# Attention beside an MLP on one core: the wide exponential of the turned head moved behind the third or fourth pair of scores

## The chip, the core and the metric

The kernel runs on one core of a Trainium2 chip. The core has five engines, each with a queue of its own that is worked off in order: PE (TensorE, matmuls), DVE (VectorE), ACT (ScalarE), POOL (GpSimd) and SP (SyncE, which here only issues DMAs). POOL and ACT issue DMAs too. Matmuls write to PSUM, eight banks of 128 x 512 float32; everything else lies in SBUF or in DRAM.

The metric is the device time of one execution in microseconds (us). The median of three runs is 1149.64 us (1147.74 to 1149.71). The profile was taken from one execution, which took 1147.51 us.

## The reference

```python
x = A_x                                   # 1 x 2048 x 448
xn = _layernorm(x, axis=-1)
# attention, 16 heads of 28, one key and one value head for all
q = (xn @ wq) ; k = xn @ wk ; v = xn @ wv
p = softmax(q k^T * 28**-0.5)             # 16 x 2048 x 2048
a = (p v) @ wo
# channel MLP: layernorm again, 448 -> 1792 -> 448
h = gelu(einsum("bsd,df->bsf", _layernorm(xn), w1) + b1)
return x + a + (einsum("bsf,fd->bsd", h, w2) + b2)
```

All data are float32. Products that need it are split into a high and a low part.

## The kernel before, in words

**Order of the whole.** First come the layer norm, the projections to q, k and v, and the MLP, with the attention's row maxima woven in (up to about 470 us). The rest of the span is the attention proper. All of it is written out by hand: the program is recorded in the order in which the Python code runs, engine by engine, and no scheduler changes that order.

**Units and steps.** The attention has 16 units u: four chunks c of 512 queries by four groups g of four heads. A unit has 8 steps, one for each pair of key tiles kt, kt + 1 (128 keys each). So there are 128 steps n, and n = 8u + kt/2.

**Two ways to compute p = exp(score).** Heads 0 to 2 of a unit (in units 0 and 1 all four) are computed with keys on the partitions. `scores` (L780 to L793) makes two matmuls of 128 x 512 into one two-bank PSUM tile `s` of a pool with two buffers, and one ACT instruction takes the exponential of both (128 x 1024, L793). That is "a pair". The maximum over keys must be known before, and is folded into the matmul as an additional row of the queries. It comes from `max_stream` (L475 on): one matmul (L485) and one DVE reduction (L486) for each 128 queries by 512 keys, 16 for each head computed so, 800 in all. These matmuls take buffers of the PSUM pool `mp`, tiles `m`, of which there are three.

Head 3 of units 2 to 15 (`TURNED`) is computed the other way round, with queries on the partitions. `turned_scores` (L736 on) makes a matmul of 128 x 512 into a tile `m` (L742); DVE scales it into the SBUF tile `raw` and takes the maximum on the way (L743). Four of these make one tile t of 128 queries by 2048 keys, and L747 joins the four maxima. `turned_exp` (L753 to L765) then takes a wide exponential in place (128 x 1024, L760; two for each tile t) and issues eight DMAs of 64 KB that put blocks of 32 x 32 in order in the tile `turned`: three from POOL's queue, five from SP's. `turn_blocks` (L767 to L770) transposes within the blocks on DVE (128 x 1024, L769) and so gives the same p, keys on the partitions, for two key tiles. A turned head has 16 turned matmuls, 8 wide exponentials and 8 transpositions. The first transposition of a unit needs the data of all eight wide exponentials.

**Value products.** `pv` (L717 on) multiplies p with v: for each key tile one matmul per head (L722), the four heads side by side in the columns. They run in bursts of two key tiles, one burst a step, and always those of the step before. At the end of a unit `norm_jobs` (L649 on) divides by the sums of the softmax, in stages that later steps call one by one (ACT, DMAs on POOL's queue, DVE, POOL). At the end of a chunk `o_jobs` (L629 on) multiplies by `wo`, 12 matmuls a step for four steps.

**The order in a step.** `ORDERS` (L28) spells it out, a string for units 0 and 1 and one for the others. Each letter is a call:

- `p`: one pair of scores. In turned units there are three pairs a step, in units 0 and 1 four.
- `m`: one maximum of `max_stream`, if the plan says that it is due. The plan spreads what is left of the 800 over the steps by `weight` (L805).
- `t`: one turned matmul with its DVE instruction, from a given step on.
- `x`: one wide exponential with its eight DMAs, if a tile t is complete.
- `T`: one transposition.
- `P`: the burst of value products.
- `e`: in a given step of a unit, `load_max`: the finished maxima of the next unit are transposed and loaded.
- `n`: one stage of `norm_jobs`. `o`: one tile of `o_jobs`.

From step 8 on the queries of a later unit (`load_q`, L447 on, DMAs L457), the queries for the maxima and for the turned heads (`load_m`, L404 on, DMAs L409) and the stages of `norm_jobs` are loaded through POOL's queue. `load_q` is called at the start of a unit's first step.

Tiles of p come from a pool of seven buffers, `turned` from one of two, `raw` from one of three.

Of the kernel before, what the change touches and what calls it, by code (L numbers as in the profile page):

```python
# [24 lines left out]
SCALE = DH ** -0.5  # L25
BURST = 2
MLP_MAX = 20
ORDERS = ("mptmpmtmpmexnPpmonm", "ptmpTeoxnPptmTn")  # L28
TURNED = tuple(range(2, 16))
RAWS = 3  # L30
LEAD = 11
# [5 lines left out]
def block_kernel(ctx, tc, x, wq, wk, wv, wo, w1, b1, w2, b2, out):  # L37
# [4 lines left out]
    def f(t):  # L42
        return t.bitcast(F32)
# [7 lines left out]
    def heads_of(u):  # L51
        return 3 if u in TURNED else 4
# [346 lines left out]
    NU = len(units)  # L399
# [16 lines left out]
    for c in range(NCH):  # L416
        center, turn = norm_parts((c + 1) % NCH, c + 1 == NCH)
        for i in range(4):
# [7 lines left out]
            if i in ((2, 3) if c == 0 else (1, 3)):  # L426
                n = 2 * c + i // 3
# [19 lines left out]
    def load_q(u):  # L447
        c, g = units[u]
        cols = slice(c * CW, (c + 1) * CW)
        if u < 2:  # L450
            qst.append(xt_p.tile([P, 4, CW], F32R, name="xh"))
            pool.memset(f(qst[u]), 0.0)
        qs = qst[u % 2]
        for blk, i in ((1, 0), (2, 0), (0, 1), (3, 1)):
            nh = heads_of(u)
            src = qd[i][4 * DH * g:4 * DH * g + DH * nh, cols].rearrange("(j r) n -> r j n", r=DH)
            loads.dma_start(f(qs[32 * blk:32 * blk + DH, 0:nh, :]), src)  # L457
        qss[u] = qs
# [5 lines left out]
    def load_max(u):  # L464
        qs, mr = qss[u], mrs.pop(u)
        nh = heads_of(u)
        pm = mtile([nh * CT, P])
        pe.transpose(pm, mr[:, 0:nh * CT], ident)
        mn = keep.tile([4 * CT, 2, P], F32R, name="mn", bufs=1)[0:nh * CT]
        act.activation(mn[:, 0, :], pm, AF.Copy, scale=-1.0)  # L470
        dve.scalar_tensor_tensor(mn[:, 1, :], pm, -1.0, f(mn[:, 0, :]), op0=ALU.mult, op1=ALU.subtract)
        loads.dma_start(f(qs[60:61, 0:nh, :]), f(mn[:, 0, :]))
        loads.dma_start(f(qs[124:125, 0:nh, :]), f(mn[:, 1, :]))
# [128 lines left out]
    def turned_tile():  # L602
        return att.tile([P, 4 * CT, CW], F32, name="turned", bufs=2)
# [14 lines left out]
    def prep_wo(g):  # L618
        act.activation(woh[:, g, :], wor[:, g, :], AF.Copy)
        pool.tensor_sub(wol[:, g, :], wor[:, g, :], f(woh[:, g, :]))  # L620
# [8 lines left out]
    def o_jobs(c, gs, tiles=range(CT)):  # L629
        last = NG - 1 in gs  # L630
        for k in tiles:
            po = mtile([P, D])
            ts = slice(k * P, (k + 1) * P)
            for g in gs:
                oth, otl = ots[c, g]
                pe.matmul(po, oth[:, ts], woh[:, g, :], start=(g == gs[0]), stop=False)  # L636
                pe.matmul(po, oth[:, ts], wol[:, g, :], start=False, stop=False)
                pe.matmul(po, otl[:, ts], woh[:, g, :], start=False, stop=(g == gs[-1]))
            a = rows[c, k]
            dve.tensor_add(a, a, po)  # L640
            if last:
                (nc.scalar if k % 2 and c == NCH - 1 else nc.sync).dma_start(ov[:, CT * c + k, :], a)
            yield
# [73 lines left out]
    def pv(u, kt):  # L717
        if kt == 0:
            pos[u] = op.tile([P, CW], F32, name="po")
        po = pos[u]  # L720
        for j in range(4):
            pe.matmul(po[32 * j:32 * j + 32, :], vs[:, kt, :], ps.pop((u, kt, j)),  # L722
                      start=(kt == 0), stop=(kt == NT - 1))
        if kt == NT - 1:
            if u == NU - 1:
                end_jobs(u, pos.pop(u))
                return
            side.add(norm_jobs(u, pos.pop(u)))
            side.step()
            c, g = units[u]  # L730
            if c < NCH - 1 and g == NG - 1:
                oside.add(o_wait(c, range(NG), range(CT)))
# [20 lines left out]
    def turned_exp():  # L753
        if not exps:
            return
        u, t, raw, m3, h = exps.pop(0)
        if u not in turned:
            turned[u] = turned_tile()
        rs = slice(2 * h, 2 * h + 2)
        act.activation(raw[:, rs], raw[:, rs], AF.Exp, bias=m3[:, 4:5], scale=1.0)  # L760
        for r in range(2 * h, 2 * h + 2):
            for a in range(4):
                q = pool if a == 3 or (a == 2 and r % 2) else nc.sync
                q.dma_start(turned[u][32 * r:32 * r + 32, 4 * t + a, :],  # L764
                            raw[32 * a:32 * a + 32, r].rearrange("p b i -> p (b i)"))  # L765

    def turn_blocks(u, kt):  # L767
        p = pair_of()
        dve.transpose(p.rearrange("p k (g j) -> p g k j", j=32),  # L769
                      turned[u][:, :, 32 * kt:32 * kt + 64].rearrange("p g (k j) -> p g k j", j=32))  # L770
        ps[u, kt, 3], ps[u, kt + 1, 3] = p[:, 0], p[:, 1]
# [8 lines left out]
    def scores(u, kt, jobs, apart):  # L780
        p = pair_of()
        if apart:
            for i, (k, j) in enumerate(jobs):
                s = mtile([P, CW])
                pe.matmul(s, ks[:, (kt + k) * P:(kt + k + 1) * P], qss[u][:, j, :], start=True, stop=True)
                act.activation(p[:, i], s, AF.Exp, scale=SCALE)
                ps[u, kt + k, j] = p[:, i]
            return
        s = sp.tile([P, 2, CW], F32, name="s")
        for i, (k, j) in enumerate(jobs):  # L790
            pe.matmul(s[:, i], ks[:, (kt + k) * P:(kt + k + 1) * P], qss[u][:, j, :], start=True, stop=True)  # L791
            ps[u, kt + k, j] = p[:, i]
        act.activation(p, s, AF.Exp, scale=SCALE)  # L793
# [7 lines left out]
    steps = [(u, kt) for u in range(NU) for kt in range(0, NT, 2)]  # L801
    pvq = [(u, kt) for u in range(NU) for kt in range(NT)]
    total = 4 * CT * len(heads)
    left = total - maxed
    weight = [0 if n >= len(steps) - LEAD else 24 if n < 6 else 18 if u < 2 else 6 for n, (u, kt) in enumerate(steps)]  # L805
    for n, (u, kt) in enumerate(steps):
        if n == 8:
            loads = pool
        if 4 <= n < 4 + NG:
            prep_wo(n - 4)  # L810
        if u + 1 < NU and kt == 0:
            load_q(u + 1)
        jobs = [((0, 0), (0, 1)), ((0, 2), (1, 2)), ((1, 0), (1, 1))]
        if u not in TURNED:
            jobs[1:2] = [((0, 2), (0, 3)), ((1, 2), (1, 3))]
        for what in ORDERS[u in TURNED]:
            if what == "p":
                scores(u, kt, jobs.pop(0), n >= len(steps) - LEAD and len(jobs) == 0)
            elif what == "m":
                if maxed < total - left + left * sum(weight[:n + 1]) / sum(weight):  # L820
                    maxed += mxs.step()
            elif what == "t":
                if n >= 8 * (TURNED[0] - 1) - 2:
                    tq.step()
            elif what == "x":
                turned_exp()
                if n == 8 * (NU - 1) - 2:
                    turned_exp()
            elif what == "T":
                if u in TURNED and (kt == 0) == (not jobs):  # L830
                    turn_blocks(u, kt)
            elif what == "e":
                if kt == (6 if u + 2 < NU else 10) and u + 1 < NU:
                    load_max(u + 1)
            elif what == "n":
                side.step()
            elif what == "o":
                if n == len(steps) - 5:
                    oside.add(o_jobs(NCH - 1, range(NG - 1)))
                oside.step()  # L840
            elif what == "P":
                for _ in range(BURST if n else 0):
                    pv(*pvq.pop(0))
    while pvq:
# [28 lines left out]
```

## Time and profile before

| | us |
|---|---|
| median of three runs | 1149.64 |
| lowest, highest | 1147.74, 1149.71 |
| profiled execution, its own time | 1147.51 |
| its span | 1145.7 |
| PE / DVE / ACT / POOL busy | 1123.2 / 900.4 / 663.3 / 505.1 |

The span runs from the first to the last instruction of the profiled execution; 1.8 us of its time lie outside it. PE has an instruction in flight for 98% of the span. As matmuls are pipelined and their ends are modelled, that share is not a measure of how much work PE could still take.

How to read the rows further on. A row of a timeline has the start in us from the span's start, the duration in us, the engine, the line, the operation, output<-input, and how many instructions were merged; the bracket gives the idle time of the engine just before and what ended it. A row of waits has the waiting engine and line, what released it, the total in us, the number of times and the longest. A row of windows has the stretch in us, its length, the busy time of the engines (with the number of instructions), the granted clock of PE as a share of full speed, the DMA share and the GB/s moved.

### The profile page before, as it was taken

How to read it: one execution, taken by the hardware profiler on the slowest of the kernel's cores; microseconds unless marked ns; L12 is line 12 of the kernel's file. 1: busy time of each engine (PE TensorE's matmuls, PEld its weight loads, DVE VectorE, ACT ScalarE, POOL GpSimd, SP SyncE). 2: the span in 40 equal slices, each digit the busy share in tenths (PEclk: the TensorE clock that was granted, in tenths of full speed). 3: DMA queues.
4: the chain of work that ended last, by engine and by line, in shares of the span. 5: the costliest groups of instructions: out<-in, count | busy, mean ns of one | idle time of the engine just before them, and what ended most of it. 6: DMA issues, size and time to landing. Idle time of an engine off the chain costs nothing.

```text
span 1145.7 us, 17740 instructions
## 1 busy us (share of the span) xinstructions
PE 1123.2 (98%) x5793; PEld 715.9 (62%) x5793; DVE 900.4 (79%) x1676; ACT 663.3 (58%) x789; POOL 505.1 (44%) x779
## 2 busy tenths in 40 slices
PE   9999999999999999999999999999999999999998
PEld 8778888888888888854444445544445444455444
DVE  7789999999999999977767776677776778776743
ACT  6753221222222111177888887778885888876883
POOL 5332341122113112314647765747874576574530
PEclk9999999999999999999999999999999999999999
DMA  8751101000100102033446575556755556664520
GB/s 275 200 189 49 56 17 58 17 17 25 49 22 20 49 25 49 17 96 76 118 112 169 138 179 144 144 128 158 178 160 143 136 141 151 170 159 124 140 62 33
DMA packets 72489, 120.06 MB, mean 105 GB/s; under 512 B 24678, under 2 KB 33572, under 8 KB 72396
## 3 DMA queue, kind: packets, MB, share of 16 engines
q1 hardware_dynamic: 49484, 74.75, 23.1%
q0 software_dynamic: 21504, 43.59, 15.2%
q8 instruction: 46, 0.75, 0.3%
q10 hardware_dynamic: 1408, 0.57, 0.2%
q14 instruction: 47, 0.39, 0.1%
HBM read 45.19 MB, written 13.88 MB: 52 GB/s over the span
## 4 chain that ended last, share of the span: by engine, by line
PE 83%; DVE 6%; DMA 4%; ACT 3%; issue 2%; POOL 2%; SPq 1%; DVEq 0%; ACTq 0%; POOLq 0%
PE po L722 18%; PE s L791 15%; PE m L485 15%; PE ph L169 9%; PE m L544 4%; PE m L542 4%; PE m L540 4%; PE m L742 3%; DVE mx L486 2%; ACT p L793 2%; DMA xh<-qd 2%; DMA turned<-raw 2%; PE qp L169 1%; PE m L636 1%; PE ph L172 1%
## 5 line engine op out<-in xcount | busy, mean ns | idle before, releaser
L486 DVE TENSOR_REDUCE mx<-m 128x1 f32<-128x512 f32 x800 | 526.7, 688 | 49.0 <-PE m L485 43.5
L793 ACT ACTIVATE p<-s 128x1024 f32<-128x1024 f32 x389 | 379.5, 1026 | 125.7 <-PE s L791 125.2
L485 PE MATMUL m<-ks,qm 128*128 128x512 f32 x800 | 321.9, 405 | 1.3 <-DVE mx L486 0.6
L722 PE MATMUL po<-p,vs 128*32 128x512 f32 x2048 | 260.0, 599 | 9.6 <-DVE p L769 9.5
L791 PE MATMUL s<-xh,ks 128*128 128x512 f32 x778 | 260.8, 419 | 2.5 <-ACT p L793 0.9
L743 DVE TENSOR_SCALAR_CACHE_REDUCE raw<-m 128x512 f32<-128x512 f32 x224 | 153.3, 684 | 116.1 <-PE m L742 102.9
L764 POOL DMA_DIRECT2D turned<-raw x336 | 168.8, 508 | 119.7 <-ACT raw L760 107.0
L791 PEld LDWEIGHTS s<-xh,ks 128*128 128x128 f32 x778 | 131.7, 188 | 140.9 <-ACT p L793 91.4
L526 ACT ACTIVATE hr<-ph,b1t 128x512 f32<-128x512 f32 x56 | 38.5, 688 | 305.5 <-PE ph L174 281.7
L531 POOL TENSOR_TENSOR hl<-hr,hh 128x512 fp32r<-128x512 f32 x56 | 72.2, 1290 | 301.6 <-PE m L485 284.5
L485 PEld LDWEIGHTS m<-ks,qm 128*128 128x128 f32 x800 | 150.2, 188 | 52.6 <-DVE raw L743 16.5
L769 DVE STREAM_TRANSPOSE p<-turned 128x1024 f32<-128x1024 f32 x112 | 138.4, 1236 | 32.6 <-DMA xh<-qd 10.3
L722 PEld LDWEIGHTS po<-p,vs 128*32 128x32 f32 x2048 | 55.1, 109 | 143.0 <-issue 118.3
L760 ACT ACTIVATE raw<-raw,m 128x1024 f32<-128x1024 f32 x112 | 127.6, 1140 | 0.0
L742 PE MATMUL m<-ks,q 128*128 128x512 f32 x224 | 88.1, 393 | 0.0
L540 PE MATMUL m<-w2h,hh 128*128 128x448 f32 x224 | 82.4, 368 | 0.0
L544 PE MATMUL m<-w2h,hl 128*128 128x448 f32 x224 | 82.0, 366 | 0.0
L542 PE MATMUL m<-w2l,hh 128*128 128x448 f32 x224 | 81.9, 366 | 0.0
L169 PE MATMUL ph<-xh,w1l 128*128 128x512 f32 x168 | 66.2, 394 | 0.0
L169 PE MATMUL ph<-xl,w1h 128*128 128x512 f32 x168 | 66.1, 393 | 0.0
L169 PE MATMUL ph<-xh,w1h 128*128 128x512 f32 x168 | 66.1, 393 | 0.0
L742 PEld LDWEIGHTS m<-ks,q 128*128 128x128 f32 x224 | 42.1, 188 | 10.6 <-DVE raw L743 0.6
(153 smaller groups left out, 1130.2 us busy)
## 6 DMA issues: line engine op xcount, KB each, us to landing
turned<-raw SPq DMA_DIRECT2D x560, 64.0 KB
turned<-raw POOLq DMA_DIRECT2D x336, 64.0 KB, 2.4
xh<-qd POOLq DMA_DIRECT2D x56, 168.0 KB, 5.0
qm<-qd SPq DMA_DIRECT2D x160, 56.0 KB
qd<-qe SPq DMA_DIRECT2D x24, 256.0 KB
tr<-ld POOLq DMA_DIRECT2D x56, 64.0 KB, 2.5
raw<-in_B_w_dram SPq DMA_DIRECT2D x7, 448.0 KB
acc<-in_A_x_dram SPq DMA_DIRECT2D x3, 896.0 KB
```

Source lines behind the costliest of these rows:

```text
L169: pe.matmul(ps, w, v, start=(n == 0), stop=False)
L485: pe.matmul(pm, qm[:, t * P:(t + 1) * P], ks[:, n * CW:(n + 1) * CW], start=True, stop=True)
L486: dve.tensor_reduce(mx[:, CT * j + t, n:n + 1], pm, axis=AX.X, op=ALU.max)
L540: pe.matmul(m2[k], hh[:, ts], w2h[:, ft, :], start=(ft == 0), stop=False)
L544: pe.matmul(m2[k], hl[:, ts], w2h[:, ft, :], start=False, stop=(ft == NF - 1))
L722: pe.matmul(po[32 * j:32 * j + 32, :], vs[:, kt, :], ps.pop((u, kt, j)), start=(kt == 0), stop=(kt == NT - 1))
L742: pe.matmul(sc, q3[i][:, t * P:(t + 1) * P], ks[:, n * CW:(n + 1) * CW], start=True, stop=True)
L743: dve.tensor_scalar(raw[:, :, 4 * n:4 * n + 4, :].rearrange("p r b i -> p b r i"), sc.rearrange("p (b r i) -> p b r i", r=4, i=32), SCALE, ...
L764: q.dma_start(turned[u][32 * r:32 * r + 32, 4 * t + a, :], raw[32 * a:32 * a + 32, r].rearrange("p b i -> p (b i)"))
L769: dve.transpose(p.rearrange("p k (g j) -> p g k j", j=32), turned[u][:, :, 32 * kt:32 * kt + 64].rearrange("p g (k j) -> p g k j", j=32))
L791: pe.matmul(s[:, i], ks[:, (kt + k) * P:(kt + k + 1) * P], qss[u][:, j, :], start=True, stop=True)
L793: act.activation(p, s, AF.Exp, scale=SCALE)
```

## The change

The order strings, the plan of the maxima and the start of the turned matmuls are changed:

```diff
-ORDERS = ("mptmpmtmpmexnPpmonm", "ptmpTeoxnPptmTn")
+ORDERS = ("mptmpmpmenPpxtmonm", "ptmpTeonPpxtmn")
...
-    weight = [0 if n >= len(steps) - LEAD else 24 if n < 6 else 18 if u < 2 else 6 for n, (u, kt) in enumerate(steps)]
+    weight = [0 if n >= len(steps) - LEAD else 24 if n < 6 else 16 if u < 2 else 6 for n, (u, kt) in enumerate(steps)]
+    first_t = 8 * (TURNED[0] - 1) - 3
...
+        after = False
...
             elif what == "t":
-                if n >= 8 * (TURNED[0] - 1) - 2:
+                if n > first_t or n == first_t and after:
                     tq.step()
             elif what == "x":
                 turned_exp()
-                if n == 8 * (NU - 1) - 2:
-                    turned_exp()
             elif what == "T":
-                if u in TURNED and (kt == 0) == (not jobs):
+                if u in TURNED:
                     turn_blocks(u, kt)
...
             elif what == "P":
+                after = True
                 for _ in range(BURST if n else 0):
                     pv(*pvq.pop(0))
```

- The wide exponential stood between the second pair and the burst in turned units (third pair in units 0 and 1), ahead of it. It now stands behind the pair that follows the burst. The stage of `norm_jobs` that followed it now precedes the burst without it.
- The transposition stood behind the second pair, but in a unit's first step at the step's end. It now stands behind the second pair in every step.
- The turned matmuls begin in step 5, with the one behind the burst, instead of step 6 with both. So a tile t is complete at the first turned matmul of a step and not at the second, and the last wide exponential of a head is issued two steps before its unit begins and not one step before. The second wide exponential in step 118 is gone.
- In units 0 and 1 the second turned matmul stands behind the fourth pair instead of ahead of the third, and there are six places for maxima in a step instead of seven. Their weight in units 0 and 1 behind step 5 is 16 instead of 18. All 800 are computed as before.

No instruction is added or removed; the work, the tiles and the DMAs are the same.

## The prediction

> **What bounds the kernel now.** I read the page first, then the waits, then the time from one burst of value products (PV, L722) to the next, step by step.
>
> ```profile
> span 1145.7 us, 17740 instructions
> PE 1123.2 (98%) x5793; PEld 715.9 (62%) x5793; DVE 900.4 (79%) x1676; ACT 663.3 (58%) x789; POOL 505.1 (44%) x779
> PE 83%; DVE 6%; DMA 4%; ACT 3%; issue 2%; POOL 2%; SPq 1%; DVEq 0%; ACTq 0%; POOLq 0%
> ```
>
> PE looks full, but matmul ends are modelled: the 98% hides waits of tenths of a microsecond. The places where PE truly stands are few, and one group leads once the MLP is over:
>
> ```profile
> PEld po L722 <- DVE p L769: 21.0, 13, 3.2
> PE po L722 <- DVE p L769: 9.5, 8, 2.3
> DVE p L769 <- DMA xh<-qd: 10.3, 6, 2.6
> ```
>
> Thirteen times a burst waits for a transposed block of the turned head (L769, called T below). One such place, at the change from unit 3 to unit 4:
>
> ```profile
> 651.93 1.92 PE L722 MATMUL po<-p,vs 128*32 128x512 f32 x16
> 652.27 1.24 DVE L769 STREAM_TRANSPOSE p<-turned 128x1024 f32<-128x1024 f32 x1
> 652.95 1.14 ACT L760 ACTIVATE raw<-raw,m 128x1024 f32<-128x1024 f32 x1
> 653.78 0.73 PE L791 MATMUL s<-xh,ks 128*128 128x512 f32 x2
> 654.61 2.96 ACT L793 ACTIVATE p<-s 128x1024 f32<-128x1024 f32 x3 [0.51 <-PE s L791]
> 654.78 0.69 DVE L743 TENSOR_SCALAR_CACHE_REDUCE raw<-m 128x512 f32<-128x512 f32 x1 [1.27 <-PE m L742]
> 656.40 2.47 POOL L457 DMA_DIRECT2D xh<-qd  x4
> 656.43 1.92 PE L722 MATMUL po<-p,vs 128*32 128x512 f32 x16
> 661.99 1.25 DVE L769 STREAM_TRANSPOSE p<-turned 128x1024 f32<-128x1024 f32 x1 [1.99 <-DMA xh<-qd]
> 663.29 1.90 PE L722 MATMUL po<-p,vs 128*32 128x512 f32 x10 [1.43 <-DVE p L769]
> ```
>
> The last wide exponential (L760, x) of unit 4's turned head ran from 652.95. SP's five copies of it were issued in 3.04 us from 654.12, but at 656.40 POOL issued the next unit's queries (L457). T, ready at 660.00 on DVE, started at 661.99, and the next burst stood until 663.29. In an ordinary step T runs 0.34 after the burst's start (652.27 against 651.93) and nobody waits.
>
> What that costs is read from the stretches between burst starts. The first two rows are of ten stretches behind a unit's first step (units 2, 3, 4, 6, 7, 8, 10, 11, 12, 14), the next two of 53 ordinary steps in twelve stretches:
>
> ```profile
> 587.25:592.59 5.34, 5.32 (x27) 1.00 0.71 105
> sum 63.85, PE 54.57; mean PE 5.46
> 592.59:619.48 26.89, 26.82 (x156) 12.50 (x155) 20.72 (x44) 23.85 (x26) 17.50 (x32) 1.00 0.45 121
> sum 237.08, PE 236.58 PEld 110.00 DVE 182.56 ACT 205.94 POOL 164.31; mean PE 19.72 PEld 9.17 DVE 15.21 ACT 17.16 POOL 13.69
> 694.66:701.60 6.94, 6.94 (x39) 4.34 (x39) 2.81 (x7) 6.67 (x8) 4.21 (x8) 1.00 0.95 214
> 701.60:709.54 7.94, 7.89 (x39) 4.32 (x38) 7.14 (x13) 3.91 (x4) 1.50 (x3) 1.00 0.41 98
> 856.10:862.91 6.81, 6.81 (x38) 4.20 (x38) 2.06 (x6) 6.53 (x8) 4.16 (x8) 1.00 0.95 209
> 862.91:871.02 8.11, 8.07 (x39) 4.46 (x38) 7.72 (x14) 4.00 (x4) 1.55 (x4) 1.00 0.42 100
> 1097.90:1101.35 3.45, 3.45 (x23) 1.46 (x23) 0.00 (x0) 3.41 (x6) 0.00 (x0) 1.00 0.45 131
> 1101.35:1106.20 4.85, 4.49 (x24) 1.58 (x23) 4.70 (x6) 3.00 (x6) 0.73 (x1) 1.00 0.01 2
> ```
>
> An ordinary step is 237.08 / 53 = 4.47. The ten boundary steps are 63.85 - 10 x 4.47 = **19.1** too long. Units 5 and 9 put output products into these steps, so I compare with the step just before: 7.94 - 6.94 and 8.11 - 6.81, **2.3**. The last unit: 4.85 - 3.45, **1.4**. Together 22.8 us stand at the boundaries. That is what the change can win.
>
> **The change, part by part.**
>
> *T of a unit's first step moves from the step's end to its middle, and x starts half a step sooner.* In the new order all T stand behind the second pair, so at a boundary it ends 0.34 + 1.24 = 1.6 behind one burst and is wanted by the next, 4.47 behind it: 2.9 to spare. Its data must be there earlier too. The turned scores start one place earlier, so the last wide exponential of a head is issued in the step two before the unit (8u - 2), not one before. It stands behind the third pair's exponential, which starts 2.68 behind the burst (654.61 against 651.93), so x runs from 3.60 (0.92 on, as from 560.47 to 561.39 below) to 4.74. From there to T's slot, two steps on, are 2 x 4.47 + 0.34 - 4.74 = 4.5 us. The copies take:
>
> ```profile
> 654.12 3.04 SPq L764 DMA_DIRECT2D turned<-raw  x5
> DMA to landing us min/median/max: 1.9/2.2/2.4
> ```
>
> The last of five is issued between 2.4 and 3.0 and lands at 4.6 to 5.4. T is then 0.1 to 0.9 late on DVE, which is idle 1.27 in front of the next turned maximum (row 654.78). So nothing behind T moves. The query load of the new unit now stands on POOL behind the copies of the step 8u - 1, and so behind the copies that T waits for; the collision above hits a head that is wanted eight steps later. Gain taken: all 22.8. Bounds: all, or none if the lateness is as now.
>
> *POOL's queue.* Its three copies of x need 1.5 and a landing, less than SP's, unless POOL is held. It is, at times:
>
> ```profile
> 768.75 1.49 POOL L671 DMA_DIRECT2D tr<-ld  x3 [2.84 <-issue]
> 775.69 1.28 POOL L681 TENSOR_TENSOR otl<-oc,oth 128x512 fp32r<-128x512 f32 x1
> 778.97 1.51 POOL L764 DMA_DIRECT2D turned<-raw  x3
> 780.47 2.02 POOL L409 DMA_DIRECT2D qm<-qd  x4
> ```
>
> In the changed program the queue loads, casts and output scaling stand ahead of a unit's last three wide copies, as they do now. In three of fourteen units four maximum loads (2.02) fall between them and the copies T needs. There T is up to 0.9 + 2.0 = 2.9 late; 1.3 is DVE's idle time, and about 0.8 more (an estimate: one reduction of 0.69, row 654.78) the three PSUM buffers of the maxima give. I take 0.7 for each, **2.0** in all (below: 0, if POOL has caught up; above: 8, if each of the units lost 0.6).
>
> The Trainium skill, page "DMA: Bandwidth & Descriptors", section "Queues, rings and completion order", says that each DMA engine takes turns between the queues it has work for, a packet at a time. The trace agrees as far as the wait of 1.99 at 661.99 goes, where the copies were issued ahead of the load. By that rule the maximum loads would also stretch the copies issued behind them in these three units, by at most that 1.99: 3 x 2.0 more, and the sum would be -10, the time 1138.
>
> *x behind the fourth pair in units 0 and 1.* Here are four pairs a step, in two PSUM buffers:
>
> ```profile
> 554.55 1.92 PE L722 MATMUL po<-p,vs 128*32 128x512 f32 x16
> 556.40 0.73 PE L791 MATMUL s<-xh,ks 128*128 128x512 f32 x2
> 557.23 2.94 ACT L793 ACTIVATE p<-s 128x1024 f32<-128x1024 f32 x3 [0.87 <-PE s L791]
> 559.81 0.63 PE L791 MATMUL s<-xh,ks 128*128 128x512 f32 x2
> 560.37 1.50 PE L722 MATMUL po<-p,vs 128*32 128x512 f32 x12
> 560.47 1.02 ACT L793 ACTIVATE p<-s 128x1024 f32<-128x1024 f32 x1 [0.30 <-PE s L791]
> 561.39 1.14 ACT L760 ACTIVATE raw<-raw,m 128x1024 f32<-128x1024 f32 x1
> 530.12:578.33 48.21, 47.89 (x248) 23.53 (x247) 34.47 (x78) 40.70 (x43) 30.31 (x55) 1.00 0.46 123
> ```
>
> Now x runs while PE is in the burst (561.39), and costs nothing. Behind the change the chain is: burst, 1.85, fourth pair's scores; its exponential starts 0.83 later (2.68) and x at 3.60; the next step's first exponential starts at 4.64 (1.14 less the 0.10 by which two overlap) and ends at 5.66. The third pair takes the buffer that this one empties, and all three pairs stand ahead of the next burst. So its scores start at about 5.7 at the earliest, and the burst 0.56 later (559.81 to 560.37, two matmuls) plus one more matmul, a maximum's, 0.28: a step of 6.6. The last row is of eight such steps, 6.03 each. Eight steps have an x in this place: 8 x 6.6 - 48.2 = **+4.6**. Below: 0, if PE's other order saves what the chain adds; above: 7, at 6.9 a step. In the turned units only two pairs precede the burst; the second waits for the third pair's exponential, which comes ahead of x, and ACT still has its 0.51 idle (row 654.61), so x's new place costs nothing. Without that idle time each of 104 steps would lose a tenth or so.
>
> *The maxima.* 800 as before. From the orders, steps 5 and 6 have one more each, the first step two fewer, and two move behind unit 1. At about 0.3 us the long steps' share cancels; **+0.2**.
>
> *The tail.* The double x in step 118 becomes single. ACT is the bound there (3.41 of 3.45, row 1097.90), so up to 1.0 could be won; taken as 0, since x in steps 117 and 118 now delays the pair behind it.
>
> **Sum.** -22.8 + 2.0 + 4.6 + 0.2 = -16.0. The profiled execution took 1147.51, so 1131.5; the median of the runs before is 1149.64, by which it would be 1133.6. I say 1132.
>
> **The rivals.**
>
> 1. *Slower: T's new slot is too early.* T at a boundary waits in the middle of DVE's queue, with the turned maximum, the maxima, and behind them PE, held by three PSUM buffers. It decides once the copies land more than 2.1 us behind the slot (1.3 idle plus 0.8 buffers); each further microsecond then costs 14 boundaries x 1. Break-even is 18.0 / 14 = 1.3 beyond, 3.4 late. At 4.3 late: -18.0 + 14 x 2.2 = +12.8, **1160**. For it: POOL's hold of 2.84, and copies at 778.97 that lag. Against it: SP's copies are unhindered and the load now follows. Chance 0.11.
> 2. *Part of it:* 2.9 late in most units, so 0.7 x 14 = 10 given back, **1141**. Chance 0.12.
> 3. *The turned steps lengthen,* as ACT's idle time is gone: 0.1 x 104 = 10, **1142**. Against it stands the 0.51. Chance 0.06.
> 4. *The change doesn't do what it says:* the copies stay as late as now, no boundary gains, and the long steps cost 0 to 4.8: 1147.5 to **1152**. Chance 0.05.
> 5. *The long steps hide x:* -16.0 - 4.6, **1127**. Chance 0.08.
>
> **How the numbers follow.** The forecast has 0.58. The range goes from 1123 (no cost at all: 1124.7, and a little of the tail) to 1147, with rivals 2, 3 and 5 inside. The median of this kernel can tell about 0.2% from no change. Faster: 0.58 + 0.12 + 0.06 + 0.08 = 0.84; within 0.2%: 0.04, most of rival 4; slower: 0.11 and the rest of rival 4, 0.12.
>
> **What would show it.** Right: bursts waiting for L769 fall from 21.0 and 9.5 to below 4 and 1; the ten boundary stretches come to some 46 instead of 63.85; T in a unit's first step starts 0.3 to 1.3 behind the burst; the eight long steps grow from 48.2 to some 53; ordinary steps stay at 4.47. Wrong: DVE waits of over 2 us at T with PE idle behind L742 or L485 (rival 1), ordinary steps over 4.55 (rival 3), long steps still at 6.0 (rival 5).

## The result and the profile after

The median after is 1140.28 us (1139.12 to 1140.40, four runs), beside 1148.69 us (1146.86 to 1149.71, four runs) for the kernel before on the same chip. The ratio is 0.9926, with a 95% interval of 0.9909 to 0.9944. The change makes the kernel faster, by 8.4 us, which is about half of what was forecast. The time lies in the range.

The page of the kernel after, its span, its engines and its chain:

```profile
span 1138.6 us, 17698 instructions
PE 1112.8 (98%) x5793; PEld 713.3 (63%) x5793; DVE 897.7 (79%) x1676; ACT 656.3 (58%) x789; POOL 503.4 (44%) x779
PE 79%; DVE 6%; ACT 5%; DMA 4%; issue 2%; POOL 2%; SPq 0%; DVEq 0%; ACTq 0%; POOLq 0%
```

The profiled execution took 1140.35 us, so 7.2 less than the one before, and its span is 7.1 shorter. The counts of the engines are equal; the 42 instructions fewer are of the kinds that are not counted as busy. Nothing on this page says where the time was won. The view of waits of the kernel after says more (engine and line, releaser, total in us, times, longest):

```profile
PEld s L791 <- ACT p L793: 110.2, 153, 1.3
...
DVE p L769 <- DMA turned<-raw: 11.4, 6, 3.8
...
DVE rc L666 <- DMA rc<-oc: 4.1, 3, 1.7
```

The group that led before, bursts waiting for T (L769), 21.0 and 9.5 us, is no longer among them. Two new ones stand there: T waits for its own copies, and the reciprocals of the softmax sums (L666, one stage of `norm_jobs`) wait for a DMA. PE's loads of weights wait more for ACT (110.2; it was 91.4).

The stretches between burst starts show what each is worth. First the kernel before, for the two wholes that were not shown yet (step 16 to 116, then step 1 to 7), and the first step of unit 6:

```profile
582.75:1082.32 499.57, 489.02 (x2712) 236.40 (x2711) 362.37 (x744) 402.53 (x425) 313.68 (x566) 1.00 0.58 149
493.83:530.12 36.29, 35.65 (x186) 17.52 (x185) 24.85 (x45) 25.04 (x30) 4.62 (x4) 1.00 0.22 52
741.91:746.27 4.36, 4.36 (x27) 1.95 (x26) 1.77 (x5) 4.36 (x6) 3.73 (x8) 1.00 0.81 208
```

Then the kernel after. The sum is of the ten stretches behind a unit's first step, in the same ten units as before; the other rows are the two wholes, the eight long steps, the first steps of units 5, 6 and 9, those behind 5 and 9, and the last unit's:

```profile
592.84:597.44 4.60, 4.60 (x28) 2.14 (x27) 3.43 (x7) 4.06 (x5) 4.23 (x8) 1.00 0.86 218
...
sum 44.93, PE 44.81 PEld 20.29 DVE 35.77 ACT 37.96 POOL 27.73; mean PE 4.48 PEld 2.03 DVE 3.58 ACT 3.80 POOL 2.77
588.42:1075.74 487.32, 480.82 (x2716) 234.97 (x2715) 362.67 (x749) 397.98 (x426) 316.49 (x574) 1.00 0.61 155
493.83:530.91 37.08, 35.52 (x186) 17.71 (x185) 24.80 (x46) 25.07 (x29) 4.57 (x4) 1.00 0.22 53
530.91:583.84 52.93, 46.87 (x244) 23.11 (x243) 33.21 (x75) 39.56 (x44) 28.14 (x51) 1.00 0.38 104
697.90:705.51 7.61, 7.09 (x38) 4.13 (x37) 5.22 (x11) 6.49 (x8) 6.12 (x11) 1.00 0.76 190
705.51:712.58 7.07, 7.07 (x39) 4.39 (x38) 4.29 (x8) 3.89 (x4) 1.49 (x3) 1.00 0.61 125
744.38:750.32 5.94, 4.63 (x27) 2.14 (x26) 3.22 (x6) 5.62 (x7) 4.76 (x9) 1.00 0.64 173
853.96:863.43 9.47, 7.07 (x39) 4.35 (x38) 5.38 (x10) 6.63 (x8) 6.59 (x14) 1.00 0.79 191
863.43:870.28 6.85, 6.84 (x38) 4.20 (x37) 3.69 (x7) 3.89 (x4) 2.08 (x4) 1.00 0.40 97
1094.67:1098.68 4.01, 4.01 (x23) 1.68 (x22) 3.98 (x6) 3.00 (x6) 0.72 (x1) 1.00 0.00 0
```

From these rows the 7.1 us of the span are put together. The starts and ends of the stretches also give step 15 and all behind step 116:

| place | before | after | difference | forecast |
|---|---|---|---|---|
| ten stretches behind a first step | 63.85 | 44.93 | -18.92 | -19.1 |
| those of units 5 and 9 | 16.05 | 13.92 | -2.13 | -2.3 |
| first steps of units 5, 6, 9 (6.94, 4.36, 6.81 before) | 18.11 | 23.02 | +4.91 | +2.0 |
| the rest of steps 16 to 115 | 401.56 | 405.45 | +3.89 | 0 |
| eight long steps | 48.21 | 52.93 | +4.72 | +4.6 |
| steps 1 to 6, and 15 | 40.71 | 41.66 | +0.95 | +0.2 |
| behind step 116 | 63.38 | 62.86 | -0.52 | -1.4 |
| sum | | | -7.10 | -16.0 |

The row of the rest is the whole less the three rows above it (499.57 - 98.01 and 487.32 - 81.87).

**The late T.** The start of unit 9 in the kernel after. First its POOL timeline:

```profile
846.72 1.28 POOL L674 TENSOR_TENSOR oc<-oc,tr 128x512 f32<-128x512 f32 x1 [1.75 <-DMA tr<-ld]
847.96 2.05 POOL L409 DMA_DIRECT2D q<-qd  x4
850.03 0.63 POOL L680 TENSOR_SCALAR oth<-oc 128x512 fp32r<-128x512 f32 x1
850.75 1.29 POOL L681 TENSOR_TENSOR otl<-oc,oth 128x512 fp32r<-128x512 f32 x1
851.98 4.46 POOL L764 DMA_DIRECT2D turned<-raw  x9
```

and rows of the other engines in the same timeline:

```profile
848.63 1.14 ACT L760 ACTIVATE raw<-raw,m 128x1024 f32<-128x1024 f32 x1
...
858.20 1.25 DVE L769 STREAM_TRANSPOSE p<-turned 128x1024 f32<-128x1024 f32 x1 [3.81 <-DMA turned<-raw]
...
860.09 0.50 PE L485 MATMUL m<-ks,qm 128*128 128x512 f32 x1 [2.40 <-DVE raw L743]
```

The last wide exponential of unit 9's head ends at 849.77. POOL is busy until 851.98 with the loads of a later turned head's queries (`q`, L409) and the output's scaling (L674 to L681), and then has nine copies in hand, three each of three exponentials. Those that T needs are the middle three, issued by 854.95, 5.2 behind the exponential's end. T was ready on DVE at 854.39 and starts at 858.20. The maxima behind it on DVE come late, and PE stands for 2.40 us.

At units 5 and 6 T waits 2.16 and 2.72. There POOL had issued the three copies 3.8 and 3.1 behind the exponential's end; at units 7 and 13, whose first steps did not grow, it was 3.6 and 3.4. What sets units 5 and 6 apart is the time from the issue of a copy to its landing. For POOL's three copies at unit 6, then at unit 9, it is:

```profile
DMA to landing us min/median/max: 4.1/4.4/4.4
DMA to landing us min/median/max: 3.3/3.5/3.8
```

At unit 5 it is 3.4 to 3.6, at units 7 and 13 it is 2.5 to 2.7, and the median of all copies from POOL is 2.3. The three of unit 6 stand right behind four maximum loads (739.84 to 741.84).

**The reciprocal.** In the kernel after, two rows of the timeline of step 27:

```profile
631.22 0.72 POOL L663 DMA_DIRECT2D rc<-oc  x1
639.44 0.25 DVE L666 RECIPROCAL rc<-rc 128x16 f32<-128x16 f32 x1 [1.70 <-DMA rc<-oc]
```

and its stretch:

```profile
638.20:643.91 5.71, 5.16 (x28) 2.06 (x27) 4.43 (x11) 5.07 (x7) 4.32 (x10) 1.00 0.62 166
```

The step is 1.2 longer than its like. Steps 99, 19 and 51 are longer too, by 0.6, 0.3 and 0.2: together 2.3 of the 3.9. Most of what is left is 15 more turned steps that take about 4.58 and not 4.50 (20 between 4.55 and 4.65, and 5 before). Thirteen of the 20 are odd steps with two maxima, in which the turned matmul behind the burst is now the first of a tile t and no longer the last. Before, such steps took 4.49 to 4.51.

### The profile page after: what moved, and what is told of

Its sections match the earlier page's. It is cut to its first block, busy times and chain, and to the rows that moved or that the text cites. A ratio compares the mean times of both kernels' runs of the same rounds, so it can differ in the third digit from the quotient of the medians.

```text
span 1138.6 us, 17698 instructions
## 1 busy us (share of the span) xinstructions
PE 1112.8 (98%) x5793; PEld 713.3 (63%) x5793; DVE 897.7 (79%) x1676; ACT 656.3 (58%) x789; POOL 503.4 (44%) x779
## 4 chain that ended last, share of the span: by engine, by line
PE 79%; DVE 6%; ACT 5%; DMA 4%; issue 2%; POOL 2%; SPq 0%; DVEq 0%; ACTq 0%; POOLq 0%
PE po L722 17%; PE m L485 15%; PE s L791 15%; PE ph L169 9%; PE m L544 4%; PE m L542 4%; PE m L540 4%; PE m L742 3%; ACT p L793 3%; DMA turned<-raw 3%; DVE mx L486 2%; ACT raw L760 2%; PE qp L169 1%; PE m L636 1%; PE ph L172 1%
## 5 line engine op out<-in xcount | busy, mean ns | idle before, releaser
L722 PE MATMUL po<-p,vs 128*32 128x512 f32 x2048 | 247.0, 598 | 0.0
L791 PEld LDWEIGHTS s<-xh,ks 128*128 128x128 f32 x778 | 132.1, 188 | 145.6 <-ACT p L793 110.2
L769 DVE STREAM_TRANSPOSE p<-turned 128x1024 f32<-128x1024 f32 x112 | 138.3, 1235 | 28.6 <-DMA turned<-raw 11.4
L742 PEld LDWEIGHTS m<-ks,q 128*128 128x128 f32 x224 | 42.1, 188 | 11.8 <-DVE mn L471 1.5
```

The source lines that it names most:

```text
L742: pe.matmul(sc, q3[i][:, t * P:(t + 1) * P], ks[:, n * CW:(n + 1) * CW], start=True, stop=True)
L769: dve.transpose(p.rearrange("p k (g j) -> p g k j", j=32), turned[u][:, :, 32 * kt:32 * kt + 64].rearrange("p g (k j) -> p g k j", j=32))
```

## The experiments

Eight kernels were run, each beside the kernel before, which had a median of 1147.11 in the first four and of 1147.28 in the last four. All are edits of the kernel after, but for the third.

### 1. The long steps back

```diff
-ORDERS = ("mptmpmpmenPpxtmonm", "ptmpTeonPpxtmn")
+ORDERS = ("mptmpmtmpmexnPpmonm", "ptmpTeonPpxtmn")
...
-                if n > first_t or n == first_t and after:
+                seen += 1
+                if n > first_t or n == first_t and seen == 2:
```

> Theory A: the wide exponential behind the fourth pair puts itself between that pair's exponential and the next first one, and so sets the long steps of units 0 and 1 (6.6 us each, 52.9 for eight). With the old order in units 0 and 1 alone and the turned units as in the changed kernel they go back to about 6.0 each: 4.7 us less, 1135.6. Rival: they are longer because of the re-dealt maxima (six places instead of seven, weight 16): they stay near 6.6, 1140.

Measured: 1132.00 (1131.42 to 1133.93), ratio 0.9865 (0.9837 to 0.9893). The eight long steps:

```profile
529.83:577.71 47.88, 47.07 (x244) 22.98 (x243) 32.39 (x75) 40.70 (x44) 28.53 (x52) 1.00 0.46 123
```

They fall back by 5.05, so the order of units 0 and 1 costs what the chain through ACT said. The edit brings the seventh place for maxima back as well; but the eight steps hold as many matmuls here as in the kernel after (244 in both rows), so it is not the number of maxima. Steps 1 to 6 win another 1.2. Most of the rest comes from unit 9, whose first step is 6.95 long here; why this edit, which does not touch it, heals it was not tried, but POOL's queue is filled in another rhythm now. Unit 13 became late instead (7.95 for 6.94).

### 2. The transposition of a first step at its end, as before

```diff
-ORDERS = ("mptmpmpmenPpxtmonm", "ptmpTeonPpxtmn")
+ORDERS = ("mptmpmpmenPpxtmonm", "ptmpTeonPpxtmTn")
...
-                if u in TURNED:
+                if u in TURNED and (kt == 0) == (not jobs):
```

> The changed kernel, but the transposition of a unit's first step stands at the step's end again. Theory A: the data are there in time, so no wait for copies is left at the boundaries (DVE waits at the transposition under 2 us in all but the last unit), but the transposition ends too late for the burst: some 0.9 us at each of 11 boundaries, as at unit 2 before (5.34 against 4.47), +10, and the lateness in units 5, 6 and 9 (4.7 us) is gone: 1145.5. Rival: only the time of the data matters and the place does not: 1136.

Measured: 1140.35 (1139.92 to 1141.79), ratio 0.9941 (0.9917 to 0.9965): the same as the change, between the two times expected (1145.5 and 1136). The sum of the ten stretches of this kernel, in its view of windows:

```profile
sum 52.25, PE 52.13 PEld 21.53 DVE 47.64 ACT 38.73 POOL 32.17; mean PE 5.21 PEld 2.15 DVE 4.76 ACT 3.87 POOL 3.22
```

and the bursts' wait for T, in its view of waits:

```profile
PEld po L722 <- DVE p L769: 6.4, 11, 0.7
```

So of the 18.9 won there, 11.6 come from earlier data alone (63.85 to 52.25) and 7.3 from T's place. But with T at the end no first step is late (6.81, 4.51 and 6.94 in units 5, 6, 9), and that is worth 4.8. In this kernel T's new place wins hardly more than it loses.

### 3. The kernel before, with T in the middle of every step

```diff
-                if u in TURNED and (kt == 0) == (not jobs):
+                if u in TURNED and jobs:
```

> The kernel before, with the transposition of a unit's first step moved to the middle of the step and nothing else. Theory A: the copies land 4.4 to 7.9 us behind the exponential's end and the new slot is 2.6 behind it, so DVE stands 2 to 5 us at nearly every boundary, holding maxima and turned scores: no gain or a loss, 1145 to 1160, say 1151. Rival: the place of the transposition alone brings the gain: boundary stretches near 4.5, 1128 to 1135.

Measured: 1173.27 (1171.60 to 1183.30), ratio 1.0240 (1.0189 to 1.0291): slower, by far more than expected. T's waits on DVE:

```profile
DVE p L769 <- DMA xh<-qd: 27.3, 7, 4.8
DVE p L769 <- DMA turned<-raw: 14.8, 4, 5.4
```

and its windows, first steps 16 to 116, then the first step of unit 5, 12.90 long, in small stretches:

```profile
582.26:1106.51 524.25, 494.47 (x2712) 241.64 (x2711) 361.38 (x744) 402.62 (x425) 312.65 (x566) 0.97 0.55 142
...
697.00:698.00 1.00, 0.14 (x1) 0.00 (x0) 0.00 (x0) 1.00 (x2) 1.00 (x2) 1.00 1.01 242
698.00:699.00 1.00, 0.00 (x0) 0.00 (x0) 0.46 (x1) 0.03 (x1) 0.11 (x1) 1.00 1.08 240
699.00:700.00 1.00, 0.00 (x0) 0.00 (x0) 1.00 (x2) 0.00 (x0) 0.00 (x0) 0.57 1.18 182
...
699.14:705.97 6.83, 5.54 (x14) 4.79 (x15) 4.20 (x8) 2.06 (x2) 1.49 (x3) 0.50 0.26 39
```

This is rival 1: T stands in the middle of DVE's queue without its data, 42.1 us in all, and PE with it. The first row shows what was not reckoned with: the granted clock is 0.97 over 524 us. In the small stretches it is the third number from the end. PE stands from 697.14 to 700.43, 3.29 us, and then works at half clock for 5.54 (last row), mostly on twelve output products in a row. Three per cent of 524 us (0.97 is rounded, so 2.5 to 3.5) are 13 to 18 us of full clock, an upper bound for what this adds to the 24.7 that the stretch is longer.

### 4. The maximum loads through SP's queue

```diff
-            loads.dma_start(f(qm[32 * blk:32 * blk + DH, :]),
+            (loads if qm_given else nc.sync).dma_start(f(qm[32 * blk:32 * blk + DH, :]),
```

`qm_given` is true for the queries of the turned heads, whose loads stay on POOL's queue.

> The changed kernel, but the queries for the maxima are loaded through SP's queue instead of POOL's. Theory A: the three late boundaries (first steps of units 5, 6 and 9: 7.61, 5.94 and 9.48 us) come from four such loads that stand on POOL ahead of the copies: they shrink to about 6.9, 4.5 and 7.0, 4.7 us less, 1135.6. Rival: POOL is held by the scaling's loads, product and casts and not by these four: at most 1 us gained, 1139.5; or SP's copies of the wide exponential are pushed back in turn, 1141.

Measured: 1139.27 (1136.75 to 1142.82), ratio 0.9919 (0.9896 to 0.9942): no gain. Units 5, 6 and 9 are better (7.45, 5.13, 6.94 in their first steps), but unit 13, which was not late, now is. Its POOL timeline (lines are one higher in this kernel):

```profile
1001.64 2.04 POOL L410 DMA_DIRECT2D q<-qd  x4
1003.70 0.63 POOL L681 TENSOR_SCALAR oth<-oc 128x512 fp32r<-128x512 f32 x1
1004.42 1.29 POOL L682 TENSOR_TENSOR otl<-oc,oth 128x512 fp32r<-128x512 f32 x1
1005.64 2.51 POOL L765 DMA_DIRECT2D turned<-raw  x5
1009.82 0.50 POOL L765 DMA_DIRECT2D turned<-raw  x1 [1.67 <-issue]
```

and stretches of unit 13's first step in its windows:

```profile
1011.64:1013.86 2.22, 0.00 (x0) 0.00 (x0) 1.89 (x4) 1.92 (x2) 2.22 (x5) 1.00 0.58 153
...
1014.80:1018.00 3.20, 3.20 (x10) 2.85 (x10) 2.12 (x5) 1.02 (x1) 2.04 (x4) 0.51 0.93 214
```

The maximum loads were one part of what holds POOL; the other loads, the scaling and a stall of 1.67 (put down to "issue") do it as well. The stall stands ahead of the third copy that T needs, the 492nd DMA that POOL issues; the last section says why that number matters. PE stands 2.22 here and the clock falls to 0.51 for some three microseconds: the step is 3.91 longer than the 6.94 of the kernel after. The execution profiled took 1140.06 with a mean granted clock of 0.998; of the seven, the four with 1.000 took 1136.75 to 1139.27.

### 5 and 6. The wide exponential ahead of the burst again

Number 5 in the turned units alone, number 6 in all (with the counter of number 1):

```diff
-ORDERS = ("mptmpmpmenPpxtmonm", "ptmpTeonPpxtmn")
+ORDERS = ("mptmpmpmenPpxtmonm", "ptmpTeoxnPptmn")
```

```diff
-ORDERS = ("mptmpmpmenPpxtmonm", "ptmpTeonPpxtmn")
+ORDERS = ("mptmpmtmpmexnPpmonm", "ptmpTeoxnPptmn")
```

> The changed kernel, but in the turned units the wide exponential stands ahead of the burst again; the turned matmuls still start in step 5 and the transposition stays in the middle. Theory A: what makes the data early is the earlier start of the turned matmuls (a whole step at the boundary); the new place of the wide exponential gives 2.6 us of that back. So the boundary stretches stay at 44.9 us for ten, the transpositions that SP's copies make wait are free, those that POOL holds remain: 1137 to 1140. Rival: the place behind the pair is needed, because ahead of the burst the wide exponential waits for the joined maximum (L747) in every second step and delays the third pair: ordinary steps grow by 0.1 or more, 1145 and over.

> The same, and units 0 and 1 in the old order too, so that of the change only the earlier start of the turned matmuls, the transposition in the middle and the weight of the maxima are left. Theory A: the gains of the two add, 1132.0 less 0 to 3: 1129 to 1132. Rival as for the run before: 1137.

Measured: number 5, 1134.45 (1134.15 to 1136.74), ratio 0.9887 (0.9860 to 0.9915); number 6, 1128.54 (1127.14 to 1131.57), ratio 0.9835 (0.9806 to 0.9865). The place of x behind the pair, which gives the change its name, is not what brings the gain: without it the kernel is some 4 us faster (number 5 beside the kernel after 12.8 for 8.4 us, number 6 beside number 1 18.7 for 15.1, each against the kernel before of its own session). Number 5 lies below both times that were expected for it. Its profiled span is 3.6 shorter than that of the kernel after: 1.5 of it lies behind step 116, 1.4 in the first step of unit 6. What is left of the change in number 6 is the earlier start of the turned matmuls, T's place, the weight of the maxima and the single x in step 118. Steps 27, 99, 19 and 51 take 4.49 to 4.51 in both; the wait for the sums is 0.8 us in number 6, and in number 5 it has gone to step 59 (1.96 us there, and the step takes 5.37). In both, units 5 and 9 are still late (8.67 and 8.50 in number 6).

### 7 and 8. All queries of `load_m` through SP's queue

Number 7 is number 1, number 8 is number 6, each with:

```diff
-            loads.dma_start(f(qm[32 * blk:32 * blk + DH, :]),
+            nc.sync.dma_start(f(qm[32 * blk:32 * blk + DH, :]),
```

> Units 0 and 1 in the old order (1132.0 without the rest), and all loads of queries for maxima and turned heads through SP. Theory B: the transpositions that still come late (units 5, 6, 9 or 13) are held by POOL's queue as a whole, four-load groups, turned queries and casts in one line; with eight loads a unit gone from it no first step is over 5.0 (7.2 with output products): 4 us less, 1128. Rival: SP has no room and its copies get late instead: 1132 or over.

> Both together: wide exponentials ahead of the burst everywhere, turned matmuls from step 5, transposition in the middle, all such loads through SP. Theories A and B: no boundary waits are left, 1126 to 1128. Rival: 1131 or over, if one queue's relief is the other's load.

Measured: number 7, 1130.88 (1130.36 to 1132.38), ratio 0.9854 (0.9827 to 0.9881), hardly better than number 1: unit 6 stays late (6.20), and step 91 is 8.58 long, at a clock of 0.81: there the reciprocal of the sums waits 4.41 for its DMA, and PE stands for 1.71. Number 8, **1125.27** (1124.66 to 1125.87), ratio 0.9801 (0.9771 to 0.9832), is the fastest of all. Its POOL timeline at the start of unit 9:

```profile
835.03 1.51 POOL L764 DMA_DIRECT2D turned<-raw  x3
836.58 0.63 POOL L680 TENSOR_SCALAR oth<-oc 128x512 fp32r<-128x512 f32 x1
837.29 1.30 POOL L681 TENSOR_TENSOR otl<-oc,oth 128x512 fp32r<-128x512 f32 x1
838.53 1.54 POOL L764 DMA_DIRECT2D turned<-raw  x3
```

and its windows, steps 16 to 116 and the eight long steps:

```profile
582.46:1062.78 480.32, 478.69 (x2716) 235.41 (x2715) 361.11 (x747) 404.06 (x426) 277.87 (x497) 1.00 0.64 156
530.12:578.04 47.92, 47.08 (x245) 22.95 (x244) 32.37 (x75) 40.68 (x44) 22.17 (x39) 1.00 0.47 123
```

The copies that T needs are out by 840.07, and T starts at 844.37 without a wait. The first steps of units 5, 6, 9 and 13 take 6.88, 4.51, 6.95 and 6.95. In steps 16 to 116, PE is busy for 478.69 of 480.32, against 480.82 of 487.32 in the kernel after.

## Why the prediction came out as it did

The direction and the mechanism of the gain were right; the gain was about half of the one forecast. The profiled spans lack 8.9 us of the 16.0: 3.9 in ordinary steps, 2.9 through POOL's hold, 0.9 behind step 116, 0.7 for the maxima, and small differences in the other terms. The time lies in the range, which was wide enough for that (1123 to 1147).

- **Boundaries, -22.8: right.** The ten stretches came to 44.93, and 46 was given as the sign; units 5 and 9 gave 2.1 of 2.3; the last unit 0.8 of 1.4 (4.85 to 4.01), of which 0.5 is left behind step 116. The bursts' waits for L769 are gone. T in a first step starts 0.8 to 1.8 behind the burst in ten units, 2.7 in the last and 3.0 to 4.2 in units 5, 6 and 9, where the sign was 0.3 to 1.3. Experiment 2 divides the ten: 11.6 for the earlier data, 7.3 for T's place.
- **Long steps, +4.6: right, by its chain.** They grew by 4.7, and experiment 1 takes 5.05 off. In a step that starts at 550.73, x starts at 554.33 (3.60 behind, as worked out) and the next step's first exponential at 555.37 (4.64, as worked out).
- **POOL's hold, +2.0: the mechanism was right, its size was not; it measured +4.9.** The step took T 2.9 late, and 2.1 of that free of charge. T's waits were 2.16, 2.72 and 3.81, and the three steps grew by 0.67, 1.58 and 2.66, so only 1.1 to 1.5 of each wait was free. The first of the two covers, DVE's idle time of 1.3, is there; the second, 0.8 for the PSUM buffers, is not. (By the covers the sum should also have had 0.8, not 0.7, for each unit.) Four maximum loads stood right ahead of T's copies at unit 6 alone; at units 5 and 9 it was the queries of a turned head, the scaling and three earlier copies. And the sum let the copies land after the usual 2.2, while they took 3.4 to 3.6, 4.1 to 4.4 and 3.3 to 3.8 in units 5, 6 and 9. In units 5 and 6 that made much of T's lateness, as the comparison with units 7 and 13 shows. The rule of the Trainium skill's page "DMA: Bandwidth & Descriptors" (section "Queues, rings and completion order") on turns between the queues had given the prediction a stretch of at most 1.99 behind the maximum loads, and a sum of -10. At unit 6 POOL's copies did land some 2 later than the usual 2.2. But these loads stand in the same queue as the copies, so turns between queues are not shown by it. At unit 9 the hold did most: the copies were issued only by 854.95, 5.2 behind the exponential's end where 1.8 is usual. What stretched the copies of units 5 and 9 stays open.
- **"Ordinary steps stay at 4.47": wrong, +3.9.** Here the prediction counted x's own cost on ACT, and found none, but left out what the edit does to the stage of `norm_jobs` beside it. The DMA of the sums (L663) goes through POOL's queue, among the copies, and the reciprocal (L666) that waits for it stands on DVE ahead of the maxima. With x ahead again the wait is 0.8 us in experiments 6 and 8, and those four steps are of ordinary length. That it is x's place in POOL's queue, and not the earlier call of the stage, was not tried apart, and experiment 5, which has x ahead in the turned units too, still waits 1.96 in step 59. So the cause of these waits is in part open. The other part, the steps of 4.58, stays in experiment 8 (19 such steps), so it is not x's place. Every kernel that starts the turned matmuls earlier has it; experiment 3, which starts them as before, has its odd steps with two maxima at 4.49 to 4.52. Why they take 0.08 more is open.
- **Maxima, +0.2**: +0.9 in steps 1 to 6 and 15.
- **The rivals.** Rival 2's time, 1141, was measured, but not by its mechanism: three units were late, not most. Rival 3 (all turned steps a tenth longer) would have shown as 10 us, and the rest of these steps grew by 3.9, much of it in four steps. Rival 5 falls by the long steps, rival 4 by the boundaries. Rival 1 came true in three units (its sign, waits of T over 2 us with PE idle, is there) and not in the others, because the data are earlier; experiment 3 takes that away and has it at nearly every boundary, and dearer than the 1 us for 1 us that was reckoned, as the clock falls too.

## What to carry to other kernels

An instruction that waits for DMAs can go to an earlier place in its engine's queue only where the slowest of the queues that carry its data has them there in every unit; the worst unit is to be looked for, not the typical one, and what is free of charge is the idle time measured on that engine, not buffers added to it. When an operation that issues DMAs moves, list everything that it now stands ahead of or behind on the issuing queue, small DMAs with a waiting reader above all. Here the gain lay in the earlier start of the chain and in T's place, which needs it, and keeping the rest of the order as it had been, with loads taken off the loaded queue, more than doubled it (22.0 for 8.4 us, each against the kernel before of its own session).

## What the runs showed of the hardware that was not expected

A stand of PE of some two microseconds can cost twice: the granted clock falls to 0.50 and stays there for 3.41 us, in one case for 6.83. It fell behind stands of 1.71 us (experiment 7, step 91), 2.22 (experiment 4) and 2.24 to 4.83 (experiment 3, at seven boundaries); it did not fall behind 2.40 us in the kernel after and 2.32 in the kernel before. So the length alone does not decide. What does decide shows when each span is cut into windows of 3.413 us, counted back from its last fall of the clock. The first three falls of experiment 3, at 699.14, 791.30 and 832.26, lie 92.16 and 40.96 us apart, which is 27 and 12 such windows; the other five lie whole numbers of them further on. In all ten kernels the clock fell at the end of every window in which PE was idle for 1.88 us or more (19 of them, with the one at the end of each span), and of none in which it was idle for 1.61 or less. Four windows, the first two from experiment 7, then one from experiment 3 and one from the kernel after:

```profile
943.15:946.56 3.41, 1.41 (x8) 0.66 (x5) 1.81 (x6) 2.13 (x4) 1.02 (x2) 1.00 0.72 159
946.56:949.97 3.41, 3.41 (x11) 1.72 (x14) 3.41 (x9) 1.36 (x2) 2.06 (x4) 0.50 0.36 87
620.64:624.05 3.41, 1.80 (x8) 1.07 (x7) 2.52 (x5) 2.03 (x3) 3.17 (x7) 1.00 0.89 192
855.85:859.27 3.42, 1.84 (x11) 1.19 (x7) 1.07 (x1) 3.37 (x5) 3.14 (x7) 1.00 0.74 201
```

PE is idle for 2.00 in the first, and the next window has half the clock. It is idle for 1.61 in the third and 1.58 in the fourth, and the clock does not fall. The stand of 2.40 us lies across the end of the fourth window, with 0.82 of it behind. The Trainium skill, page "TensorE: Matmul & The Clock Gate", section "What's actually happening", puts the fall to half rate behind an idle window of about 3.4 us that runs freely and does not start with the stand. The half rate agrees with the 0.50, its window with the 3.41, and the whole numbers with a window that runs freely; that 1.88 to 2.24 us of idle time in it suffice does not fit a window that has to be idle throughout.

POOL's own stalls ahead of a DMA, put down to "issue" (1.67 in experiment 4, 2.60 at 863.31 in the kernel after), come at other instructions from kernel to kernel, but ahead of the same DMAs by number. In all ten kernels POOL is idle for at least 1.5 us ahead of the 129th, the 250th, the 371st and the 492nd DMA that it issues, 121 apart, and every stall of over 1.2 us that the profile puts down to "issue" on POOL behind 480 us is one of these. An edit that takes DMAs off POOL's queue moves these stalls: in experiment 4, with 40 fewer, the 492nd is a copy that unit 13 needs at once. What causes them stays open.
